# Attention with sinks and a feed-forward layer on one core: key tiles with embedded sinks, one matmul shape, a written weave

## The chip, the cores and the metric

The kernel runs on one core of a Trainium2 chip. The metric is the device time of one execution in microseconds; lower is better. TensorE multiplies matrices into PSUM (eight banks), ScalarE applies functions, VectorE does elementwise work, Pool (GpSimd) does elementwise work on SBUF alone, and SyncE (SP) issues transfers.

## The reference

There are 4 batches of 8 heads with 768 positions and 64 dimensions. Heads 0, 2 and 6 (retrieval) attend to all earlier positions; the other five (streaming) attend to the first 4 positions (the sink) and to the last 64. The attention output, 3072 tokens by 512, goes through a feed-forward layer with a PReLU of one slope per hidden feature:

```
scores = q @ k.T / 8                       # masked: causal, or causal and (sink or window)
a = exp(scores - max) / sum                # per row
x = (a @ v), heads side by side            # 3072 x 512
h = x @ w_in                               # 3072 x 2048
g = max(h, 0) + alpha * min(h, 0)
out = g @ w_out                            # 3072 x 512
```

## The kernel before

The work goes by batch and, in a batch, by four pairs of heads (0,1), (2,3), (4,5), (6,7). `att_load` brings q, k and v of the next pair (SP queue), casts q on ScalarE, k and v on VectorE. `att_pair` transposes q and k (`do_transpose`, L103), so that the two heads of a pair lie on partitions 0 to 63 and 64 to 127. `att_scores` makes transposed scores for each tile of 128 keys: TensorE multiplies 64 partitions of keys by 64 of queries (L118, L138), ScalarE takes the exponential (L120, L140), and a triangular or window mask is multiplied in, on Pool for retrieval heads (L122), on VectorE for streaming heads (L142). A streaming head has its four sink keys apart: two matmuls with 4 key columns (L128) and an exponential of 4 partitions (L130).

`att_av` multiplies by v, which carries a column of ones, into 65 columns for each query tile: full 128-key tiles (L155, L163), for streaming heads also the sink with 4 partitions (L158) and the previous key tile with 64 query columns (L161). VectorE takes the reciprocal of the sum (L166), and ScalarE or VectorE scales (L168, L171). `bridge_gen` transposes the attention output of a batch into `xT` (L211).

The feed-forward layer goes by six chunks of 512 tokens (`moe_chunk_gen`): 16 steps of four matmuls of 512 columns (L234), a scaled copy on ScalarE (L238) and a maximum on VectorE (L239); then four steps of 16 matmuls (L244), a copy (L247) and a store. It has two PSUM banks. The order is partly written and partly found: after each step of attention one step of the feed-forward queue is added, chunk 0 during batch 1, chunks 1 and 2 during batch 2, chunk 3 during batch 3, chunks 4 and 5 at the end; the framework then schedules what is ready, by priority. The weights come first, as fp32 through one staging tile, and VectorE casts them.

Of the kernel before, what the change touches and what calls it, by code (L numbers as in the profile page):

```python
# [9 lines left out]
ALU = mybir.AluOpType  # L10
# [4 lines left out]
def kernel(  # L15
# [18 lines left out]
    NB = S // 128  # L34
# [24 lines left out]
    mwin = const.tile([128, 192], bf16)
    nc.vector.memset(mwin, 1.0)  # L60
    nc.gpsimd.affine_select(mwin, mwin, pattern=[[1, 192]], base=0,
                            channel_multiplier=-1, compare_op=ALU.is_ge, fill=0.0)
    nc.gpsimd.affine_select(mwin, mwin, pattern=[[-1, 192]], base=(WIN - 1),
                            channel_multiplier=1, compare_op=ALU.is_ge, fill=0.0)
    mwin0 = const.tile([128, 192], bf16)
    nc.vector.tensor_copy(mwin0, mwin)
    nc.vector.memset(mwin0[0:NSINK, :], 0.0)

    w_in_b = wpool.tile([128, 4, d_ff], bf16)
    w_out_b = wpool.tile([128, 16, d_model], bf16)  # L70
    alpha_sb = wpool.tile([128, 16], fp32)
    tmpf = wpool.tile([128, 4096], fp32, tag="tmpf")
    for hh in range(2):
        nc.sync.dma_start(tmpf.rearrange("p (a f) -> p a f", a=4),
                          moe_w_in[:, hh * 1024:(hh + 1) * 1024].rearrange("(a p) f -> p a f", p=128))
        nc.vector.tensor_copy(
            w_in_b[:, :, hh * 1024:(hh + 1) * 1024],
            tmpf.rearrange("p (a f) -> p a f", a=4))
# [9 lines left out]
    xT = xpool.tile([128, 4, n_tok], bf16)

    def load_nat(src, key, cvt_eng):  # L90
        nat = qk.tile([128, NB, 2, 64], fp32, tag=f"nat_in_{key}")
        natb = qk.tile([128, NB, 128], bf16, tag=f"nat_b_{key}")
        for hh in range(2):
            nc.sync.dma_start(nat[:, :, hh, :], src[hh].rearrange("(i p) d -> p i d", p=128))
        cvt_eng(natb.rearrange("p i (h d) -> p i h d", h=2), nat)  # L95
        return natb

    def do_transpose(natb, dstT, psum_cvt, bank):
        for half in range(2):
            pt = ps.tile([128, 384], bf16, tag=f"b{bank + half}")  # L100
            for j in range(3):
                i = half * 3 + j
                nc.tensor.transpose(pt[:, j * 128:(j + 1) * 128], natb[:, i, :], ident)  # L103
            psum_cvt(dstT[:, half * 384:(half + 1) * 384], pt)

    def att_scores(hh, h, qT, kT, eT, eTsink):
        retr = RETR[h]
        qTh = qT[hh * 64:(hh + 1) * 64, :]
        kTh = kT[hh * 64:(hh + 1) * 64, :]
        if retr:  # L110
            for j in range(NB):
                W = S - 128 * j
                nh = (W + 383) // 384
                for g in range(nh):
                    w0 = 128 * j + g * 384
                    ww = min(384, S - w0)
# [189 lines left out]
```

## Time and profile before

| what | value |
|---|---|
| median of 3 runs | 422.54 us (420.62 to 426.4) |
| profiled execution, first to last instruction (span) | 420.2 us |
| TensorE busy | 354.1 us (84%) |
| ScalarE busy | 229.3 us (55%) |
| VectorE busy | 193.4 us (46%) |
| Pool busy | 37.4 us (9%) |

The span is the profiled execution's own time; the profile gives no other time for that execution. Busy time of an engine is the union of its instructions. Matmuls are pipelined, so the time from one start to the next is shorter than the length of a matmul, and a TensorE that is always busy need not be at its peak.

### The profile page before, as it was taken

Reading aid. Unit: us, or ns where it says so; the run is one execution under the profiler, and the core shown is the slowest. Engines: PE = TensorE matmul, PEld = TensorE weight load, DVE = VectorE, ACT = ScalarE, POOL = GpSimd, SP = SyncE. Lnnn points to the kernel's source line nnn. Section 1 sums busy time; section 2 is a strip of 40 time slices with the busy share of each in tenths; the row PEclk is TensorE's granted clock in tenths of the full one; section 3 lists DMA queues with packets and bytes.
Section 4 is the critical chain, followed back from the end, with each engine's and each line's share of the span. In section 5 each row is a group of like instructions: output and inputs, shape, how many; then the busy total and the mean of one; then the engine's idle time right before and its main releaser. Section 6 shows DMA issues by size and latency. Waiting matters only on the chain.

```text
span 420.2 us, 5539 instructions
## 1 busy us (share of the span) xinstructions
PE 354.1 (84%) x1890; PEld 156.7 (37%) x1916; DVE 193.4 (46%) x640; ACT 229.3 (55%) x581; POOL 37.4 (9%) x101
## 2 busy tenths in 40 slices
PE   0086788889899788998999999799998998798786
PEld 0033334443335344442343433434344443343332
DVE  3246555546732555665227731567614445512520
ACT  0254566658753565787438753578725565513521
POOL 1020101002010020022000020010300010000000
PEclk9999999999999555898999999799998558999999
DMA  8997975452411551124016051200011000011001
GB/s 230 284 267 220 227 136 114 112 128 62 96 44 75 112 107 30 41 52 114 25 75 114 5 135 50 64 0 2 0 53 50 0 2 0 0 51 50 1 27 75
DMA packets 83692, 33.92 MB, mean 81 GB/s; under 512 B 77520, under 2 KB 77520, under 8 KB 83664
## 3 DMA queue, kind: packets, MB, share of 16 engines
q1 hardware_dynamic: 83664, 33.57, 31.8%
q8 instruction: 15, 0.25, 0.2%
q14 instruction: 13, 0.11, 0.1%
HBM read 27.27 MB, written 6.29 MB: 80 GB/s over the span
## 4 chain that ended last, share of the span: by engine, by line
PE 73%; DVE 10%; ACT 9%; DMA 4%; issue 3%; POOL 1%; ACTq 0%; DVEq 0%
PE po L244 20%; PE psg L234 17%; PE psc L118 6%; PE psc L138 6%; PE pav L155 4%; PE pav L163 4%; PE pav L161 4%; DMA tmpf<-in_moe_w_in_dram 4%; PE pav L158 4%; DVE g L239 4%; ACT hal L238 4%; PE pt L211 3%; PE psc L128 3%; PE pt L103 2%; ACT eTr L120 1%
## 5 line engine op out<-in xcount | busy, mean ns | idle before, releaser
L234 PE MATMUL psg<-xT,w_in_b 128*128 128x512 bf16 x364 | 106.8, 397 | 11.5 <-DVE g L239 10.4
L244 PE MATMUL po<-w_out_b,g 128*128 128x512 bf16 x378 | 89.4, 380 | 1.3 <-DVE g L239 1.0
L239 DVE TENSOR_TENSOR g<-psg,hal 128x512 bf16<-128x512 f32 x96 | 65.7, 686 | 43.9 <-ACT hal L238 43.2
L238 ACT ACTIVATE hal<-psg,alpha_sb 128x512 f32<-128x512 f32 x96 | 66.0, 688 | 32.5 <-PE psg L234 27.8
L166 DVE RECIPROCAL rcp<-pav 128x1 f32<-128x1 f32 x192 | 31.0, 166 | 90.9 <-PE pav L163 51.8
L120 ACT ACTIVATE eTr<-psc 128x384 bf16<-128x384 f32 (+2 forms) x108 | 42.8, 419 | 23.8 <-PE psc L118 22.8
L234 PEld LDWEIGHTS <-w_in_b 128*128 128x128 bf16 x384 | 34.4, 101 | 46.7 <-issue 23.9
L244 PEld LDWEIGHTS <-g 128*128 128x128 bf16 x384 | 34.9, 98 | 41.5 <-issue 3.4
L122 POOL TENSOR_TENSOR eTr<-eTr,mcaus 128x128 bf16<-128x128 bf16 x72 | 32.1, 446 | 201.8 <-ACT eTr L120 201.8
L247 ACT COPY ot<-po 128x512 f32<-128x512 f32 x24 | 14.0, 585 | 62.2 <-PE po L244 53.4
L103 PE MATMUL pt<-ident,natb 128*128 128x128 bf16 x192 | 24.5, 257 | 26.2 <-ACT natb L95 14.1
L142 DVE TENSOR_TENSOR eTs<-eTs,mwin 128x192 bf16<-128x192 bf16 (+1 forms) x120 | 28.6, 249 | 38.6 <-ACT eTs L140 36.2
L140 ACT ACTIVATE eTs<-psc 128x192 bf16<-128x192 f32 (+1 forms) x120 | 36.8, 320 | 15.3 <-PE psc L138 13.1
L118 PE MATMUL psc<-qT,kT 64*128 64x384 bf16 (+2 forms) x108 | 35.5, 349 | 5.1 <-ACT eTr L120 3.8
L138 PE MATMUL psc<-qT,kT 64*128 64x192 bf16 (+1 forms) x120 | 32.2, 289 | 3.3 <-ACT eTsink L130 1.3
L168 ACT ACTIVATE xnat<-pav,rcp 128x64 bf16<-128x64 f32 x96 | 29.8, 314 | 8.0 <-DVE rcp L166 7.0
L155 PE MATMUL pav<-vb,eTr 128*128 128x65 bf16 x252 | 26.2, 215 | 2.0 <-POOL eTr L122 0.8
L211 PE MATMUL pt<-ident,xnat 128*128 128x128 bf16 x96 | 22.0, 273 | 6.6 <-ACT xT L215 4.7
L103 PEld LDWEIGHTS <-natb 128*128 128x128 bf16 x192 | 15.6, 114 | 31.0 <-ACT natb L95 14.3
L158 PE MATMUL pav<-vb,eTsink 4*128 4x65 bf16 x120 | 23.3, 216 | 4.1 <-DVE xnat L171 3.5
L163 PE MATMUL pav<-vb,eTs 128*128 128x65 bf16 x120 | 26.4, 221 | 0.0
L171 DVE TENSOR_SCALAR xnat<-pav,rcp 128x64 bf16<-128x64 f32 x96 | 25.3, 269 | 1.6
(36 smaller groups left out, 247.5 us busy)
## 6 DMA issues: line engine op xcount, KB each, us to landing
nat<-in_q_dram SPq DMA_DIRECT2D x32, 192.0 KB, 3.2
nat<-in_k_dram SPq DMA_DIRECT2D x32, 192.0 KB, 3.6
vnat<-in_v_dram SPq DMA_DIRECT2D x16, 384.0 KB, 3.7
out_dram<-ot SPq DMA_DIRECT2D x24, 256.0 KB, 2.0
tmpf<-in_moe_w_in_dram SPq DMA_DIRECT2D x2, 2048.0 KB, 8.1
tmpf<-in_moe_w_out_dram SPq DMA_DIRECT2D x2, 2048.0 KB, 9.3
alpha_sb<-in_moe_alpha_dram SPq DMA_DIRECT2D x1, 8.0 KB, 8.4
```

What stands on the lines that cost most here:

```text
L103: nc.tensor.transpose(pt[:, j * 128:(j + 1) * 128], natb[:, i, :], ident)
L118: nc.tensor.matmul(psc[:, 0:ww], kTh[:, 128 * j:128 * (j + 1)], qTh[:, w0:w0 + ww], start=True, stop=True)
L120: nc.scalar.activation(eT[j][:, g * 384:g * 384 + ww], psc[:, 0:ww], AF.Exp, scale=scale)
L138: nc.tensor.matmul(psc[:, 0:W], kTh[:, 128 * j:128 * (j + 1)], qTh[:, 128 * j:128 * j + W], start=True, stop=True)
L140: nc.scalar.activation(eT[j][:, 0:W], psc[:, 0:W], AF.Exp, scale=scale)
L155: nc.tensor.matmul(pav, eT[j][:, 128 * (i - j):128 * (i - j) + 128], vbh[:, j, :], start=(j == 0), stop=(j == i))
L158: nc.tensor.matmul(pav, eTsink[:, 128 * i:128 * (i + 1)], vbh[0:NSINK, 0, :], start=True, stop=False)
L163: nc.tensor.matmul(pav, eT[i][:, 0:128], vbh[:, i, :], start=False, stop=True)
L234: nc.tensor.matmul(psg, w_in_b[:, ci, 128 * fj:128 * (fj + 1)], xT[:, ci, t * 512:(t + 1) * 512], start=(ci == 0), stop=(ci == 3))
L238: nc.scalar.activation(hal, psg, AF.Copy, scale=alpha_sb[:, fj:fj + 1])
L239: nc.vector.tensor_tensor(g[:, fj, :], psg, hal, op=ALU.max)
L244: nc.tensor.matmul(po, g[:, fj, 128 * s4:128 * (s4 + 1)], w_out_b[:, fj, :], start=(fj == 0), stop=(fj == 15))
```

## The change

The kernel's body is rewritten. What it computes stays the same.

- All matmuls use the full array. Each of a pair's two heads has its own key tile `kT` with zeros on the other head's 64 partitions, and both use the same `qT`.
- Query tiles start at 0, 128, 252, ... (124 apart, seven of them). Key tiles of a streaming head start 124 apart, and their first four rows are overwritten with the four sink keys (and values), so that sink and window are one matmul; the mask says what counts. A streaming head has 7 score matmuls and 13 value matmuls, a retrieval head 11 and 27.
- Scores of a retrieval head are packed into six pieces of 456 columns, one exponential each; those of a streaming head into three pieces of 384. VectorE multiplies by all masks.
- All seven query tiles of a head are normalised by one reciprocal and one multiplication on VectorE. q, k and the output are evacuated from one transposition bank by VectorE alone.
- q, k and v are cast on Pool, two pairs ahead, and loaded three pairs ahead. The weights are loaded and cast by eight transfers issued from Pool, after the casts of the first two pairs.
- The PReLU is ScalarE's Relu of the negative, then one VectorE instruction (neg times 1 minus alpha, plus h). It has three PSUM banks.
- The order is written out and kept (`manual_schedule`): pieces of attention, and behind them, in equal shares, units of feed-forward: four first-layer matmuls with their two passes, or a quarter of a second-layer sum. Batch 1 gets chunk 0, batch 2 chunk 1 and the first layer of chunk 2, batch 3 the rest of chunks 2 and 3; then chunk 4's first layer, chunk 5's first layer in turn with chunk 4's second, and chunk 5's second.

The added code, cut to its core (what it replaces stands above; setting up masks and buffers is left out):

```diff
+    QS = [0] + [124 * i + 4 for i in range(1, NT)]
+    RW = [S - QS[j] for j in range(6)]
+    RB = [0, 456, 912, 1368, 1824, 2280, RTOT]
+    SLOT = 256
...
+    def load(p):
+        b, c = divmod(p, 4)
+        s = p % NF
+        ha, hb = PAIRS[c]
+        base = (b * H + ha) * S * D
+        nc.sync.dma_start(
+            qf[s].rearrange("p h i d -> p (h i) d"),
+            ap2(q, base, [[D, 128], [128 * D, 12], [1, D]]))
+        for src, dst in ((k, kf[s]), (v, vf[s])):
+            for hh, h in enumerate((ha, hb)):
+                o = (b * H + h) * S * D
+                step = 128 if RETR[h] else 124
+                nc.sync.dma_start(dst[:, 0:6, hh, :], ap2(src, o, [[D, 128], [step * D, 6], [1, D]]))
+                if not RETR[h]:
+                    nc.sync.dma_start(dst[0:24, 6, hh, :], ap2(src, o + 744 * D, [[D, 24], [1, D]]))
...
+        natq[p] = work.tile([128, 6, 128], bf16, tag="qb", name="qb")
+        natk[p] = work.tile([128, 7, 128], bf16, tag="kb", name="kb")
+        nc.gpsimd.tensor_copy(natq[p].rearrange("p i (h d) -> p h i d", h=2), qf[s])
+        nc.gpsimd.tensor_copy(natk[p], kf[s].rearrange("p i h d -> p i (h d)"))
+        nc.gpsimd.tensor_copy(vb[r][:, :, :, 0:D], vf[s])
+        for hh, h in enumerate(PAIRS[c]):
+            if not RETR[h]:
+                kh = natk[p][0:NSINK, :, 64 * hh:64 * hh + 64]
+                nc.gpsimd.tensor_copy(kh[:, 1:7, :], kh[:, 0:1, :].to_broadcast([NSINK, 6, 64]))
+                vh = vb[r][0:NSINK, :, hh, 0:D]
+                nc.gpsimd.tensor_copy(vh[:, 1:7, :], vh[:, 0:1, :].to_broadcast([NSINK, 6, 64]))
...
+    load(0)
+    load(1)
+    load(2)
...
+        nc.vector.memset(kTs[i][0][64:128, :], 0.0)
+        nc.vector.memset(kTs[i][1][0:64, :], 0.0)
...
+    cast(0)
+    cast(1)
+    for n in range(4):
+        nc.gpsimd.dma_start(w_in_b[:, :, 512 * n:512 * (n + 1)],
+                            moe_w_in[:, 512 * n:512 * (n + 1)].rearrange("(a p) f -> p a f", p=128))
+    for n in range(4):
+        nc.gpsimd.dma_start(w_out_b[:, 4 * n:4 * n + 4, :],
+                            moe_w_out[512 * n:512 * (n + 1), :].rearrange("(a p) f -> p a f", p=128))
+    def transposed(nat, n, evac):
+        tr = ps.tile([128, 1024], bf16, tag="tr", name="tr")
+        for i in range(n):
+            nc.tensor.transpose(tr[:, 128 * i:128 * (i + 1)], nat[:, i, :], ident)
+        evac(tr)
+    def Tq(p):
+        transposed(natq[p], 6, lambda tr: nc.vector.tensor_copy(qT[p % NK][:, 0:S], tr[:, 0:S]))
+    def Tk(p):
+        def evac(tr):
+            for hh in range(2):
+                rows = slice(64 * hh, 64 * hh + 64)
+                nc.vector.tensor_copy(kTs[p % NK][hh][rows, :], tr[rows, 0:896])
+        transposed(natk[p], 7, evac)
...
+        lo, hi = RB[n], RB[n + 1]
+        sc = ps.tile([128, 512], fp32, tag=f"sc{n % 2}", name="sc")
+        done = []
+        for j in range(6):
+            a, z = max(lo, RO[j]), min(hi, RO[j] + RW[j])
+            if a < z:
+                c = QS[j] + a - RO[j]
+                nc.tensor.matmul(sc[:, a - lo:z - lo], kt[:, 128 * j:128 * (j + 1)],
+                                 qt[:, c:c + z - a], start=True, stop=True)
+            if lo < RO[j] + RM[j] <= hi:
+                done.append(j)
+        nc.scalar.activation(e[:, lo:hi], sc[:, 0:hi - lo], AF.Exp, scale=scale)
+        for j in done:
+            ej = e[:, RO[j]:RO[j] + RM[j]]
+            nc.vector.tensor_tensor(ej, ej, mr[:, j, 0:RM[j]], op=ALU.mult)
...
+        parts = [(2 * n, 0, 192), (2 * n + 1, 192, 192)] if n < 2 else \
+            [(4, 0, 192), (5, 192, 148), (6, 340, 44)]
+        for j, o, w in parts:
+            nc.tensor.matmul(sc[:, o:o + w], kt[:, 128 * j:128 * (j + 1)],
+                             qt[:, 124 * j:124 * j + w], start=True, stop=True)
+        ev = e[:, 0:6 * SLOT].rearrange("p (s c) -> p s c", c=SLOT)
+        nc.scalar.activation(ev[:, 2 * n:2 * n + 2, 0:192],
+                             sc[:, 0:384].rearrange("p (s c) -> p s c", c=192), AF.Exp, scale=scale)
+        nc.vector.tensor_tensor(ev[:, 2 * n:2 * n + 2, 0:192], ev[:, 2 * n:2 * n + 2, 0:192],
+                                ms[:, 2 * n:2 * n + 2, :], op=ALU.mult)
+    def AV(p, hh):
+        h = PAIRS[p % 4][hh]
+        e, vv = ebuf.pop((p, hh)), vb[p % NV]
+        pav = ps.tile([128, NT, D + 1], fp32, tag=f"pav{hh}", name="pav")
+        for i in range(NT):
+            if RETR[h]:
+                terms = [(RO[j] + QS[i] - QS[j], j) for j in range(min(i, 5) + 1)]
+            elif i == 0:
+                terms = [(0, 0)]
+            else:
+                own = SLOT * i + 4 if i < 6 else 5 * SLOT + 152
+                terms = [(SLOT * (i - 1) + 128, i - 1), (own, i)]
+            for n, (o, j) in enumerate(terms):
+                nc.tensor.matmul(pav[:, i, :], e[:, o:o + 128], vv[:, j, hh, :],
+                                 start=(n == 0), stop=(n == len(terms) - 1))
+        if hh == 0:
+            xn[p] = work.tile([128, NT, 128], bf16, tag="xn", name="xn")
+        rcp = work.tile([128, NT, 1], fp32, tag=f"rcp{hh}", name="rcp")
+        nc.vector.reciprocal(rcp, pav[:, :, D:D + 1])
+        nc.vector.tensor_tensor(xn[p][:, :, 64 * hh:64 * hh + 64], pav[:, :, 0:D],
+                                rcp.to_broadcast([128, NT, D]), op=ALU.mult)
+    def X(p):
+        b, c = divmod(p, 4)
+        nat = xn.pop(p)
+        tr = ps.tile([128, 1024], bf16, tag="tr", name="tr")
+        for i in range(NT):
+            nc.tensor.transpose(tr[:, QS[i]:QS[i] + 128], nat[:, i, :], ident)
+        nc.vector.tensor_copy(xT[:, c, b * S:(b + 1) * S], tr[:, 0:S])
+    n_mm = [0]
+    def mm_bank():
+        n_mm[0] += 1
+        return ps.tile([128, 512], fp32, tag=f"mm{n_mm[0] % 3}", name="mm")
+    def P1(t, f):
+        psg = mm_bank()
+        for c in range(4):
+            nc.tensor.matmul(psg, w_in_b[:, c, 128 * f:128 * (f + 1)], xT[:, c, 512 * t:512 * (t + 1)],
+                             start=(c == 0), stop=(c == 3))
+        neg = work.tile([128, 512], fp32, tag="neg", name="neg", bufs=3)
+        nc.scalar.activation(neg, psg, AF.Relu, scale=-1.0)
+        nc.vector.scalar_tensor_tensor(g_buf[t % 2][:, f, :], neg, oma[:, f:f + 1], psg,
+                                       op0=ALU.mult, op1=ALU.add)
+    po = {}
+    def P2(t, s, quarter):
+        if quarter == 0:
+            po[t] = mm_bank() if t < 4 else ps.tile([128, 512], fp32, tag=f"sc{s % 2}", name="po")
+        for f in range(4 * quarter, 4 * quarter + 4):
+            nc.tensor.matmul(po[t], g_buf[t % 2][:, f, 128 * s:128 * (s + 1)], w_out_b[:, f, :],
+                             start=(f == 0), stop=(f == 15))
+        if quarter == 3:
+            ot = work.tile([128, 512], fp32, tag="ot", name="ot", bufs=3)
+            nc.scalar.copy(ot, po.pop(t))
+            nc.sync.dma_start(out[t * 512 + s * 128:t * 512 + (s + 1) * 128, :], ot)
...
+        seq = [sa[0]] + prev + sa[1:3] + tail + sa[3:5] + nxt[:1] + sa[5:] + nxt[1:] + [sb[0]]
+        seq += [lambda: AV(p, 0)] + sb[1:]
+        return seq
...
+    plan = {1: p1_units(0) + p2_units(0), 2: p1_units(1) + p2_units(1) + p1_units(2),
+            3: p2_units(2) + p1_units(3) + p2_units(3)}
+        pieces = []
+        for p in range(4 * b, 4 * b + 4):
+            pre = [lambda p=p: (load(p + 3) if p + 3 < NP else None)]
+            pre += [lambda p=p: (cast(p + 2) if p + 2 < NP else None)]
+            first = True
+            for piece in pair_pieces(p):
+                pieces.append((pre if first else [], piece))
+                first = False
+        units = plan.get(b, [])
+        lead = 5 if b else 0
+        n = len(pieces) - lead
+        given = 0
+        for i, (pre, piece) in enumerate(pieces):
+            for f in pre:
+                f()
+            piece()
+            due = len(units) * max(0, i + 1 - lead) // n
+            while given < due:
+                units[given]()
+                given += 1
+    AV(NP - 1, 1)
+    X(NP - 1)
+    for u in p1_units(4):
+        u()
+    for u, w in zip(p1_units(5), p2_units(4)):
+        u()
+        w()
+    for u in p2_units(5):
+        u()
```

## Rows read from the trace of the kernel before

**Rows 1.** Busy time and instructions by stretch, granted clock, DMA share, GB/s.

```profile
0.00:23.10 23.10, 1.64 (x12) 1.11 (x12) 7.38 (x11) 2.98 (x4) 1.59 (x9) 1.00 0.90 243
23.10:86.70 63.60, 51.78 (x271) 23.48 (x273) 35.16 (x133) 38.72 (x113) 8.80 (x23) 1.00 0.75 180
86.70:133.60 46.90, 43.90 (x235) 18.41 (x238) 21.55 (x65) 28.44 (x69) 5.46 (x14) 1.00 0.31 78
133.60:167.10 33.50, 28.07 (x173) 14.04 (x171) 18.19 (x82) 20.93 (x63) 3.65 (x9) 0.56 0.38 79
167.10:263.80 96.70, 92.61 (x496) 39.16 (x503) 46.01 (x147) 59.08 (x145) 8.82 (x23) 0.96 0.29 69
263.80:271.00 7.20, 4.79 (x43) 3.04 (x44) 4.15 (x22) 3.69 (x14) 0.00 (x0) 0.75 0.26 75
271.00:317.40 46.40, 44.24 (x243) 18.59 (x246) 22.66 (x69) 28.66 (x70) 5.97 (x14) 0.97 0.06 21
317.40:349.80 32.40, 29.39 (x174) 14.24 (x175) 15.34 (x75) 20.07 (x62) 3.08 (x9) 0.58 0.02 9
349.80:420.20 70.40, 57.66 (x254) 24.66 (x257) 23.00 (x38) 26.73 (x44) 0.00 (x0) 1.00 0.08 30
sum 420.20, PE 354.08 PEld 156.72 DVE 193.44 ACT 229.29 POOL 37.38; mean PE 39.34 PEld 17.41 DVE 21.49 ACT 25.48 POOL 4.15
```

**Rows 2.** Groups of TensorE instructions by shape, 24 to 85 us (batch 0).

```profile
L118 PE MATMUL psc<-qT,kT 64*128 64x384 bf16 x14 | 6.3, 483 | 1.2 <-ACT eTr L120 0.8 <-DVE kT L104 0.2
```

**Rows 3.** The same view, 180 to 260 us (woven).

```profile
L118 PE MATMUL psc<-qT,kT 64*128 64x384 bf16 x11 | 3.6, 343 | 1.3 <-ACT eTr L120 0.8 <-issue 0.5
```

**Rows 4.** TensorE's timeline at five places: start, length, instruction.

```profile
23.14 0.50 PE L118 MATMUL psc<-qT,kT 64*128 64x384 bf16 x1
...
28.57 0.60 PE L155 MATMUL pav<-vb,eTr 128*128 128x65 bf16 x6
...
181.09 0.35 PE L155 MATMUL pav<-vb,eTr 128*128 128x65 bf16 x6
...
188.57 0.45 PE L103 MATMUL pt<-ident,natb 128*128 128x128 bf16 x5
...
236.25 0.20 PE L158 MATMUL pav<-vb,eTsink 4*128 4x65 bf16 x1
236.38 0.22 PE L161 MATMUL pav<-vb,eTs 128*64 128x65 bf16 x1
236.53 0.20 PE L163 MATMUL pav<-vb,eTs 128*128 128x65 bf16 x1
```

**Rows 5.** By stretch: chunk 5's first layer, then its second layer, in the tail.

```profile
382.50:402.50 20.00, 14.79 (x63) 6.07 (x63) 10.37 (x15) 11.43 (x17) 0.00 (x0) 1.00 0.04 14
...
402.50:416.30 13.80, 13.70 (x63) 6.17 (x63) 0.69 (x1) 1.90 (x4) 0.00 (x0) 1.00 0.15 58
```

**Rows 6.** Groups by shape, whole span: busy us, mean ns, idle time before.

```profile
L238 ACT ACTIVATE hal<-psg,alpha_sb 128x512 f32<-128x512 f32 x96 | 66.0, 688 | 32.5 <-PE psg L234 27.8 <-DVE g L239 3.7
L239 DVE TENSOR_TENSOR g<-psg,hal 128x512 bf16<-128x512 f32 x96 | 65.7, 686 | 43.9 <-ACT hal L238 43.2
...
L122 POOL TENSOR_TENSOR eTr<-eTr,mcaus 128x128 bf16<-128x128 bf16 x72 | 32.1, 446 | 201.8 <-ACT eTr L120 201.8
...
L120 ACT ACTIVATE eTr<-psc 128x384 bf16<-128x384 f32 x60 | 28.1, 490 | 19.4 <-PE psc L118 18.9
...
L142 DVE TENSOR_TENSOR eTs<-eTs,mwin 128x192 bf16<-128x192 bf16 x100 | 24.8, 254 | 35.1 <-ACT eTs L140 32.9
...
L104 DVE COPY kT<-pt 128x384 bf16<-128x384 bf16 x32 | 10.7, 351 | 2.1 <-PE pt L103 1.8
...
L95 ACT ACT_TABLE_LOAD x1 | 1.3, 1283 | 11.9 <-DMA nat<-in_q_dram 11.9
L61 POOL TENSOR_SCALAR_AFFINE_SELECT mwin<-mwin 128x192 bf16<-128x192 bf16 x1 | 0.3, 345 | 0.0
```

**Rows 7.** Transfers by line: count, KB each, median us from issue to landing.

```profile
nat<-in_q_dram SPq DMA_DIRECT2D x32, 192.0 KB, 3.2
```

More of the change, by code (lines that the diff above doesn't have):

```diff
@@ L33 @@
     n_tok = B * S
-    NB = S // 128
     scale = 1.0 / (D ** 0.5)
@@ L59 @@
[L59 to L78, printed above, removed]
@@ L88 @@
[L88 to L104, printed above, removed]
@@ L207, in bridge_gen @@
-    def bridge_gen(b):
-        for i in range(NB):
-            for ci in range(4):
-                pt = ps.tile([128, 128], bf16, tag=f"b{ci % 2}")
-                nc.tensor.transpose(pt, x_nat[b][:, i, 128 * ci:128 * (ci + 1)], ident)
-                if ci % 2 == 0:
-                    nc.vector.tensor_copy(xT[:, ci, (b * NB + i) * 128:(b * NB + i + 1) * 128], pt)
-                else:
-                    nc.scalar.copy(xT[:, ci, (b * NB + i) * 128:(b * NB + i + 1) * 128], pt)
-            yield
@@ L251 @@
[L251 to L269 removed]
+    stat = ctx.enter_context(tc.tile_pool(name="stat", bufs=1))
@@ new lines @@
+    work = ctx.enter_context(tc.tile_pool(name="work", bufs=2))
+    ps = ctx.enter_context(tc.tile_pool(name="ps", bufs=1, space=bass.MemoryType.PSUM))
+    ctx.enter_context(tc.manual_schedule())
+    NF, NK, NV, NR, NS = 3, 2, 4, 2, 3
+    qf = [stat.tile([128, 2, 6, 64], fp32, name=f"qf{i}") for i in range(NF)]
+    kf = [stat.tile([128, 7, 2, 64], fp32, name=f"kf{i}") for i in range(NF)]
+    vf = [stat.tile([128, 7, 2, 64], fp32, name=f"vf{i}") for i in range(NF)]
+    vb = [stat.tile([128, 7, 2, 65], bf16, name=f"vb{i}") for i in range(NV)]
@@ new lines, with ap2 @@
+    qT = [stat.tile([128, S + 32], bf16, name=f"qT{i}") for i in range(NK)]
+    kTs = [[stat.tile([128, 7 * 128], bf16, name=f"kT{h}{i}") for h in range(2)] for i in range(NK)]
+    eR = [stat.tile([128, RTOT + 128], bf16, name=f"eR{i}") for i in range(NR)]
+    eS = [stat.tile([128, 6 * SLOT + 64], bf16, name=f"eS{i}") for i in range(NS)]
+    xT = stat.tile([128, 4, n_tok], bf16, name="xT")
+    g_buf = [stat.tile([128, 16, 512], bf16, name=f"g{i}") for i in range(2)]
+    def ap2(t, offset, dims):
+        return bass.AP(t.tensor, t.offset + offset, dims)
@@ new lines @@
+    nc.vector.memset(ms, 1.0)
+    for a, n in ((0, 192), (1, 44)):
+        part = ms[:, 0, :] if a == 0 else ms[:, 5, 148:192]
+        nc.gpsimd.affine_select(part, part, pattern=[[-1, n]], base=63,
+                                channel_multiplier=1, compare_op=ALU.is_ge, fill=0.0)
+        nc.vector.memset(part[0:NSINK, 0:128 if a == 0 else n], 1.0)
+        nc.gpsimd.affine_select(part, part, pattern=[[1, n]], base=0,
+                                channel_multiplier=-1, compare_op=ALU.is_ge, fill=0.0)
```

235 lines of the change are left out of this document (74 added, 161 removed).

## The prediction

> **What bounds the kernel now.** I read the page's busy shares first, then busy time by stretch, then single instructions. The nine stretches of [rows 1] are cut at the first and last feed-forward matmuls of each chunk. TensorE is busy 354.1 of 420.2 us, far more than any other engine, so the first thing to see is what that busy time consists of. Batch 0's attention has 63.6 us to itself, attention of batches 1 and 3 has 33.5 and 32.4 us to itself after its feed-forward chunk ran out, and a tail of 70.4 us has no attention.
>
> Two things in busy TensorE are not arithmetic. The first is the clock. A 64x384 score matmul takes 483 ns in batch 0 [rows 2] and 343 ns in the woven stretch [rows 3]. The granted clock reads 1.00 in batch 0, yet 483 is what the alone stretches with granted 0.56 show too; I take batch 0 to run at the lower level (1.2 GHz) and the 1.00 to be the reading ahead of the first change. The second is the change of array shape. Six matmuls of one shape, 128x65, take 0.35 us together, and one alone 0.20, so one follows another after 0.030 us; a sink, a 64-column and a full-array matmul in turn start 0.13 and 0.15 us apart [rows 4]. Every streaming head goes through these three shapes.
>
> In the tail, 16 first-layer units (four 512-column matmuls each) take 20.0 us, 1.25 each, while 63 second-layer matmuls take 13.70 us, 0.2175 each, so four are 0.87 [rows 5]. The difference is the loop matmul, ScalarE 0.69, VectorE 0.69 [rows 6] over two PSUM banks.
>
> **The change, part by part.** The sum is made against the span of 420.2; the median of the runs, 422.54, is 2.3 above, which I add at the end. A change of about 2% is what measurement can tell from none.
>
> *TensorE work of attention.* Per batch the new kernel has 80 transposes, 68 score matmuls with 13,944 columns (three full heads of 2728, five streaming heads of 1152) and 146 value matmuls of 65 columns. At 2.4 GHz: transposes at 0.06 (five in 0.45, of which the last trails by about 0.2 [rows 4]) give 4.8; the score columns 5.8, with 10 ns a matmul 6.5; the value matmuls at 0.032 give 4.7. That is 16 us a batch, and 32 at 1.2 GHz (value matmuls then 0.07: six in 0.60, less 0.23 [rows 4]). The mask of a retrieval head moves from Pool to VectorE; sinks no longer have matmuls or exponentials of their own.
>
> *Prologue.* Now the first score starts at 23.14 [rows 4], behind a weight transfer and its cast on VectorE. In the new order q, k and v of the first pair (1.18 MB) come first: at the 243 GB/s of the first stretch 4.9 us, with 3.2 us from issue to landing [rows 7] about 8. Then casts on Pool. A Pool instruction with one input took 345 ns for 192 columns, one with two inputs 446 for 128 [rows 6]; the 2560 columns of a pair's casts lie between 4.6 (at 1.8 ns) and 8.9 us (at 3.5), and I take the lower end, the row with one input, much of it fixed cost. The keys are ready some 2 us after landing, transposes and evacuation take 2.5. First score at 12.5 (11 to 18).
>
> *Batch 0.* No feed-forward covers it, as now. A pair with one retrieval head, at 1.2 GHz: nine score pieces 3.75, 20 transposes 2.5, 40 value matmuls 2.9, so about 9 us of matmul. TensorE now goes in a written order, so chains show where too little lies between: last scores, exponential (0.49 for 384 columns), mask (0.25 to 0.5), then the value matmuls of the previous head, about 1 us not covered; normalisation to transposes 0.3; evacuation of queries (0.7 by twice the 351 ns row [rows 6]) to transposes of keys 0.5; mask to the second value matmuls 0.5. That is 11.4; the pair with two streaming heads about 9. Batch 0: 43 us. At the upper clock the pairs fall to about 9, giving 34; that is the lower end. Pool (5 to 9 us a pair) stays below a pair's time.
>
> *Batches 1 to 3.* The 32, 48 and 48 units handed out cost 27.8, 41.8 and 41.8 at 0.87. With attention: 43.8, 57.8, 57.8, together 159. Do the others fit under that? VectorE in batch 2, at most: masks 18 x 0.25 + 15 x 0.51 = 12.1; evacuations (351 ns per 384 columns) 8 x 0.70 + 8 x 0.82 = 12.2; normalisation 8 x 0.77 = 6.2; second pass of the PReLU 32 x 0.69 = 22: 52.5 of 57.8. ScalarE: exponentials 17.8, first pass 22, copies 2.8: 43. So TensorE stays the bound, with VectorE close. Each piece of attention is followed by about one unit, so a chain of exponential and mask has a unit of 0.87 beside it. I add 3 us at each of three starts, where five pieces run uncovered, and 5% (8 us) for waits behind VectorE's queue: 176 (165 to 200) against 263 now (46.9+33.5+96.7+7.2+46.4+32.4).
>
> *Tail.* The last scores, mask, value matmuls, normalisation, transposes and copy leave TensorE about 3.5 us without cover. Then 64 units: with three banks a first-layer unit has 3 x 0.87 = 2.6 us for its loop of 0.87 + 0.2 + 0.69 + 0.69 = 2.45, so it runs at TensorE's rate, and chunk 5 has chunk 4's second layer beside it: 55.7. From the last matmul to the end 3.9 (416.3 to 420.2). Together 63 (61 to 70) against 70.4.
>
> Sum: 12.5 + 43 + 176 + 63 = 294.5, and with the 2.3 **297**.
>
> *Two unpriced things.* The weights come by eight transfers issued and converted by Pool, which no row shows. Beside pair 0 and 1 they cost nothing if Pool is free by about 27 us, when the third pair's casts are due; the upper bound is a rival below, and a gain below nothing is excluded, as nothing reads the weights before batch 1 (about 55 us). The second pass (scalar, tensor, PSUM) is priced like the 686 ns row of the same operands; with a per-partition pointer it may be 0.05 dearer, 1.6 us of VectorE in batch 2, under cover.
>
> **A rule weighed.** All casts go to Pool while VectorE multiplies by masks, both operands in SBUF. In the rows Pool's multiplications (446 ns) and VectorE's masks (254) ran in one kernel and the masks show no long waits on the mean [rows 6]; but Pool was busy only 37 of 420 us [rows 1]. The Trainium skill (SBUF — State Buffer, Who interferes with whom) says that a VectorE instruction with two SBUF inputs contends with a GpSimd instruction that reads SBUF, one blocking the other for its whole length; by it the sum would be some 308, by the rows 297. This is the third rival.
>
> **The rivals.**
> 1. *Upper clock in batch 0 and no loss in the weave*: minus 9 and minus 8, **280**. For it: one array shape, denser matmuls. Against: the alone stretches fell to 0.56 and 0.58 with TensorE 84 to 91% busy [rows 1]. 0.12.
> 2. *Pool is late.* The eight weight transfers stand ahead of the third pair's casts in Pool's order. If Pool is held until their 8.4 MB have moved (243 GB/s: 34 us from about 17), those casts start at 51 instead of 27: **321**. For it: Pool's order. Against: this is the far end of a cost that no row bounds from nearer. 0.13.
> 3. *Pool's reads hold up the masks.* Pool works at least 4.6 us of a pair; if half of a pair's eight masks wait half of a 1 us cast, VectorE gains 2 us a pair: 8 in batch 0, on the path, and in batch 2 60 against 57.8 of TensorE: **308**. 0.08.
> 4. *The written order waits.* The queue of before took what was ready; if the new weave gets no further than the woven stretches of before (46.9 + 96.7 + 46.4 = 190 us for 128 units, 1.48 each), batches 1 to 3 take 199: **320**. For it: VectorE 90% loaded in batch 2. Against: three banks and a unit between pieces. 0.10.
> 5. *Shape was not the price.* If streaming matmuls still start 0.14 apart, 65 x 0.11 and 35 x 0.1 us come back in each of four batches: **339**. Against it the runs of one shape in [rows 4]. 0.03.
> 6. *ScalarE reloads its table between Exp and Relu.* One load took 1283 ns [rows 6]; two for each of 64 woven first-layer units make ScalarE the bound, 73, 125 and 73 us: **408**. Before, Exp and Copy shared one load. 0.02. The Trainium skill (ScalarE: Activation LUTs, Table sets: the hidden batching unit) counts relu among the functions that stand in every set, which speaks against it; no run so far shows Relu.
> 7. *Slower: the lower clock in the woven stretches and the tail.* It falls where small matmuls prevail [rows 1]; if it stayed there from batch 1 on, 159 + 56 us would double: above **500**; it decides from 120 us of cost, a little over half of that time. Against: 1.00, 0.96 and 0.97 in the woven stretches now, where small matmuls had a larger share. 0.03.
>
> **How the numbers follow.** The forecast has 0.47, with 285 to 310 of its own; 0.02 is left for a result near the old time. From 276 to 338 hold the forecast, rivals 2 to 4 and most of rival 1: more than eight in ten, and the bounds of prologue, batch 0 and weave. Faster by over 2%: all but rival 7 and the remainder, 0.95; within 2%: 0.02; slower: 0.03.
>
> **What would show it.** Right: first score near 12.5; value matmuls of streaming heads 0.03 apart (0.07 in batch 0); nine tenths or more busy from some 55 us to the end; in the tail 64 units in 56 us, with TensorE waiting for the second pass almost never. Wrong: waits of query transposes for Pool's casts near 30 us (2), masks far above their length or VectorE busiest in batch 2 (3, 4), table loads beyond the first (6), granted clock near 0.5 after batch 0 (7). The prediction would fail most from VectorE, which has 5 us to spare in batch 2, and from Pool.

## The result and the profile after

The changed kernel takes 293.27 us (median of four, 291.89 to 294.52) against 421.58 before: a ratio of 0.693, 95% interval 0.688 to 0.699. It is 128 us faster; the forecast was 297, range 276 to 338. The profiled execution spans 290.2 us.

Busy time by stretch, kernel after; the stretches are cut at the first score, at the end of VectorE's wait for alpha, where batch 1's first scores start, at two places inside batches 1 to 3, at the last scores' value matmuls, and at the tail's first and last matmul. Columns as in [rows 1]: start and end, length, busy time (and instructions) of TensorE, of its weight loads, of VectorE, ScalarE and Pool, then the granted clock as a share of full speed, the busy share of the transfer engines, and GB/s.

```profile
0.00:12.50 12.50, 1.73 (x13) 1.30 (x13) 7.54 (x32) 1.28 (x1) 8.64 (x29) 1.00 1.11 190
12.50:30.80 18.30, 3.47 (x17) 1.83 (x18) 0.62 (x1) 3.08 (x6) 12.93 (x19) 1.00 1.34 196
30.80:60.40 29.60, 18.81 (x258) 15.33 (x257) 22.60 (x59) 12.97 (x27) 10.42 (x15) 0.88 1.13 206
60.40:110.00 49.60, 44.15 (x407) 26.66 (x414) 37.79 (x82) 25.75 (x51) 19.97 (x30) 0.97 0.62 125
110.00:170.00 60.00, 58.41 (x489) 33.32 (x495) 46.43 (x100) 37.02 (x72) 16.34 (x23) 1.00 0.61 123
170.00:228.30 58.30, 55.75 (x465) 31.74 (x472) 34.77 (x81) 29.96 (x57) 3.67 (x5) 1.00 0.09 33
228.30:230.20 1.90, 0.94 (x21) 0.80 (x20) 0.83 (x2) 0.59 (x1) 0.00 (x0) 1.00 0.10 40
230.20:286.00 55.80, 55.35 (x255) 24.98 (x257) 24.46 (x33) 23.32 (x40) 0.00 (x0) 1.00 0.10 37
286.00:290.20 4.20, 0.00 (x0) 0.00 (x0) 0.00 (x0) 0.48 (x1) 0.00 (x0) 0.83 0.17 62
```

Two things are to be seen against [rows 1]. There is no long stretch with attention alone behind batch 0 any more: from 60.4 to 286.0 TensorE is busy 214.6 of 225.6 us (the five rows from 60.4 on added up), and at full clock almost throughout. And there is a hole: from 12.5 to 30.8 it works 3.5 of 18.3 us, while the transfer engines are busy throughout (a share of 1.34; the times of packets are added up, so it can pass 1).

| stretch | before | forecast | after |
|---|---|---|---|
| to the first score | 23.1 | 12.5 | 12.5 |
| batch 0 | 63.6 | 43 | 47.9 (60.4 - 12.5) |
| batches 1 to 3 | 263.1 | 176 | 167.9 (228.3 - 60.4) |
| tail and end | 70.4 | 63 | 61.9 (290.2 - 228.3) |
| span | 420.2 | 294.5 | 290.2 |

TensorE's timeline, kernel after, at six places (start, length, instruction; in brackets the idle time ahead and what ended it). It answers to [rows 4].

```profile
32.21 0.90 PE L170 MATMUL tr<-ident,kb 128*128 128x128 bf16 x7 [15.77 <-DVE qT L174]
...
33.23 1.69 PE L245 MATMUL pav<-vb,eR 128*128 128x65 bf16 x27
...
41.35 0.98 PE L245 MATMUL pav<-vb,eR 128*128 128x65 bf16 x27
...
109.29 0.33 PE L222 MATMUL sc<-qT,kT 128*128 128x192 bf16 x2
109.45 1.03 PE L286 MATMUL mm<-w_out_b,g 128*128 128x512 bf16 x4
110.31 0.33 PE L222 MATMUL sc<-qT,kT 128*128 128x192 bf16 x3
...
111.54 0.56 PE L245 MATMUL pav<-vb,eS 128*128 128x65 bf16 x13
...
230.24 15.00 PE L272 MATMUL mm<-xT,w_in_b 128*128 128x512 bf16 x66
```

The 13 value matmuls of a streaming head take 0.56 us, 0.03 from one start to the next ((0.56 - 0.2)/12), where sink, previous tile and own tile were 0.13 to 0.15 apart. Two score matmuls of 192 columns take 0.16 before a second-layer unit starts, and that unit 0.86. In the tail, 66 first-layer matmuls run in one piece at 0.227 each.

Groups of instructions by shape, kernel after, answering to [rows 6]:

```profile
L276 DVE SCALAR_TENSOR_TENSOR g<-neg,oma,mm 128x512 bf16<-128x512 f32 x96 | 71.5, 745 | 24.8 <-ACT neg L275 22.4
L275 ACT ACTIVATE neg<-mm 128x512 f32<-128x512 f32 x96 | 57.4, 598 | 44.3 <-PE mm L272 42.9 <-DVE eS L227 0.3
...
L225 ACT ACTIVATE eS<-sc 128x384 bf16<-128x384 f32 x60 | 28.7, 489 | 45.2 <-PE sc L222 45.2
L227 DVE TENSOR_TENSOR eS<-eS,ms 128x384 bf16<-128x384 bf16 x60 | 22.5, 386 | 10.1 <-ACT eS L225 9.9
...
L180 DVE COPY kT<-tr 64x896 bf16<-64x896 bf16 x32 | 19.8, 620 | 6.1 <-PE tr L170 5.6
...
L100 POOL CAST qb<-qf 128x768 bf16<-128x768 f32 x16 | 13.2, 828 | 81.7 <-PE tr L170 73.9 <-DMA out_dram<-ot 7.8
...
L160 POOL DMA_DIRECT2D w_in_b<-in_moe_w_in_dram x4 | 3.1, 796 | 0.0
...
L209 ACT ACT_TABLE_LOAD x1 | 1.3, 1283 | 0.8 <-PEq L369 0.8
```

The second pass of the PReLU takes 745 ns (priced at 690, at most 740), the first 598. Pool casts at 828 ns for 768 columns, 1.08 ns a column, not 1.8. There is still one table load, so Relu and Exp share it.

What held VectorE (waits by releaser: total, times, longest us), kernel after:

```profile
DVE g L276 <- ACT neg L275: 22.4, 33, 1.1
DVE oma L317 <- DMA alpha_sb<-in_moe_alpha_dram: 17.7, 1, 17.7
```

The second line is the hole. VectorE takes its instructions in the order written; `oma` (1 minus alpha) stands behind the first pair's evacuations and ahead of the masks, and alpha's transfer behind the loads of three pairs in SP's queue. No step of the prediction has it.

### The profile page after: what moved, and what is told of

Its sections match the earlier page's. It is cut to its first block, busy times and chain, and to the rows that moved or that the text cites. A ratio compares the mean times of both kernels' runs of the same rounds, so it can differ in the third digit from the quotient of the medians.

```text
span 290.2 us, 5073 instructions
## 1 busy us (share of the span) xinstructions
PE 238.6 (82%) x1916; PEld 136.0 (47%) x1944; DVE 175.0 (60%) x386; ACT 134.4 (46%) x253; POOL 72.0 (25%) x118
## 3 DMA queue, kind: packets, MB, share of 16 engines
q0 software_dynamic: 4224, 4.19, 8.7%
## 4 chain that ended last, share of the span: by engine, by line
PE 64%; DVE 14%; SPq 6%; DMA 5%; POOL 5%; ACT 2%; issue 2%; POOLq 0%; ACTq 0%
PE mm L272 22%; PE mm L286 19%; PE po L286 9%; DVE g L276 6%; DMA vf<-in_v_dram 5%; SPq L85 4%; PE sc L205 4%; PE pav L245 4%; PE tr L170 3%; DVE xn L251 2%; PE tr L259 2%; PE sc L222 2%; DVE kT L180 2%; DVE eS L227 2%; DVE eR L212 2%
## 5 line engine op out<-in xcount | busy, mean ns | idle before, releaser
L272 PE MATMUL mm<-xT,w_in_b 128*128 128x512 bf16 x371 | 95.2, 381 | 1.0 <-issue 0.2
L276 DVE SCALAR_TENSOR_TENSOR g<-neg,oma,mm 128x512 bf16<-128x512 f32 x96 | 71.5, 745 | 24.8 <-ACT neg L275 22.4
L275 ACT ACTIVATE neg<-mm 128x512 f32<-128x512 f32 x96 | 57.4, 598 | 44.3 <-PE mm L272 42.9
L286 PE MATMUL mm<-w_out_b,g 128*128 128x512 bf16 x244 | 63.6, 379 | 0.6
L209 ACT ACTIVATE eR<-sc 128x456 bf16<-128x456 f32 x72 | 38.1, 547 | 32.8 <-PE sc L205 32.7
L225 ACT ACTIVATE eS<-sc 128x384 bf16<-128x384 f32 x60 | 28.7, 489 | 45.2 <-PE sc L222 45.2
L212 DVE TENSOR_TENSOR eR<-eR,mr 128x128 bf16<-128x128 bf16 (+2 forms) x72 | 19.9, 295 | 17.8 <-ACT eR L209 17.6
L286 PE MATMUL po<-w_out_b,g 128*128 128x512 bf16 x125 | 29.9, 379 | 0.1
L205 PE MATMUL sc<-qT,kT 128*128 128x456 bf16 (+8 forms) x132 | 26.0, 284 | 4.4 <-ACT eS L225 2.0
L227 DVE TENSOR_TENSOR eS<-eS,ms 128x384 bf16<-128x384 bf16 x60 | 22.5, 386 | 10.1 <-ACT eS L225 9.9
L180 DVE COPY kT<-tr 64x896 bf16<-64x896 bf16 x32 | 19.8, 620 | 6.1 <-PE tr L170 5.6
L222 PEld LDWEIGHTS <-kT 128*128 128x128 bf16 x140 | 13.1, 102 | 10.8 <-issue 1.4
L205 PEld LDWEIGHTS <-kT 128*128 128x128 bf16 x132 | 11.5, 102 | 11.4 <-issue 1.8
```

The source lines that it names most:

```text
L205: nc.tensor.matmul(sc[:, a - lo:z - lo], kt[:, 128 * j:128 * (j + 1)], qt[:, c:c + z - a], start=True, stop=True)
L209: nc.scalar.activation(e[:, lo:hi], sc[:, 0:hi - lo], AF.Exp, scale=scale)
L212: nc.vector.tensor_tensor(ej, ej, mr[:, j, 0:RM[j]], op=ALU.mult)
L222: nc.tensor.matmul(sc[:, o:o + w], kt[:, 128 * j:128 * (j + 1)], qt[:, 124 * j:124 * j + w], start=True, stop=True)
L225: nc.scalar.activation(ev[:, 2 * n:2 * n + 2, 0:192], sc[:, 0:384].rearrange("p (s c) -> p s c", c=192), AF.Exp, scale=scale)
L227: nc.vector.tensor_tensor(ev[:, 2 * n:2 * n + 2, 0:192], ev[:, 2 * n:2 * n + 2, 0:192], ms[:, 2 * n:2 * n + 2, :], op=ALU.mult)
```

## The experiments

Times are medians; differences are against the changed kernel run again beside the first three (292.5), or against the kernel before where that is the one edited. The runs were made in four groups, on different chips; the kernel before, run in each, took 421.2 to 421.8 us. In the diffs the first line of each pair is the changed kernel's, or that of the kernel before where the text says so.

### The base again

> The changed kernel once more, on the chip of the next three kernels, as their base: 293, within 1%. Its TensorE stands idle from about 16 to 32 us while VectorE waits 17.7 us for alpha.

292.5 us, ratio to before 0.694 (0.687 to 0.701). Same hole: VectorE waited 17.0 us for alpha.

### One shape of matmul: taken back in the changed kernel, and given to the kernel before

```diff
-nc.tensor.matmul(sc[...], kt[:, ...], qt[:, ...], start=True, stop=True)
+nc.tensor.matmul(sc[...], kt[64 * hh:64 * hh + 64, ...], qt[64 * hh:64 * hh + 64, ...], start=True, stop=True)
```

> The score matmuls of the changed kernel use 64 rows of the array (the half of each key tile that isn't zero) in place of 128; the other matmuls stay. Shape theory: each change between the two shapes costs about 0.1 us as in the kernel before (0.13 to 0.15 between starts where one shape needs 0.03); 132 score pieces with two changes each give 20 to 28 us of TensorE, most of it on the path in batches 1 to 3: 308 to 318. Rival (the rows cost nothing, what was saved is the count and the waits): within 2 us of 293.

313.2 us, ratio 0.740 (0.735 to 0.745): 20.7 more. TensorE's timeline of this kernel:

```profile
161.18 1.03 PE L286 MATMUL mm<-w_out_b,g 128*128 128x512 bf16 x4
162.14 0.34 PE L222 MATMUL sc<-qT,kT 64*128 64x192 bf16 x2
162.41 1.04 PE L286 MATMUL mm<-w_out_b,g 128*128 128x512 bf16 x4
```

From the unit's start to the scores' is 0.96 where it was 0.86 (109.45 to 110.31), from the scores to the next unit 0.27 where it was 0.16 (109.29 to 109.45). Each change of shape costs 0.10 us, and two changes for 132 pieces make 26; 20.7 of it comes to the end. The columns streamed are the same, so the rival falls.

The kernel before, with its value matmuls in one shape:

```diff
-nc.tensor.matmul(pav, eTsink[...], vbh[0:NSINK, 0, :], start=True, stop=False)
+nc.tensor.matmul(pav, eTsink[...], vbh[:, 0, :], start=True, stop=False)       # eTsink: 128 partitions, 124 of them zero
-nc.tensor.matmul(pav[0:64, :], eT[i - 1][:, 128:192], vbh[:, i - 1, :], start=False, stop=False)
+nc.tensor.matmul(pav, eT[i - 1][:, 128:256], vbh[:, i - 1, :], start=False, stop=False)   # eT: 64 more columns, zero
```

> The kernel before with its value matmuls in one shape: sinks multiply 128 partitions (zeros in 124), the previous key tile 128 columns (zeros in 64). As many matmuls as before, score matmuls still on 64 rows. Shape theory: 340 value matmuls start 0.03 to 0.07 after one another where they are together, in place of 0.13 to 0.17; changes to score matmuls and transposes stay: 15 to 30 us less, 392 to 407. Rival (the waits of the weave, not the shape, set the time): within 5 us of 421.6.

394.2 us, ratio 0.934 (0.927 to 0.941): 27 us less than the kernel before, with as many matmuls and more zeros multiplied. The shape of the value matmuls alone is worth, in the old schedule, as much as a fifth of the change's 128 us.

### The third PSUM bank: taken from the changed kernel, and given to the tail of the kernel before

```diff
-return ps.tile([128, 512], fp32, tag=f"mm{n_mm[0] % 3}", name="mm")
+return ps.tile([128, 512], fp32, tag=f"mm{n_mm[0] % 2}", name="mm")
```

> The first layer rotates over two PSUM banks in place of three (a second-layer sum takes its turn in the same rotation). By the loop of bank, ScalarE and VectorE (0.87 + 0.2 + 0.6 + 0.75 = 2.4 us for two units), the 16 units of chunk 4 alone take 1.2 each, 5 us more; the woven stretches have 1.1 us from one unit to the next and lose 0 to 0.3 a unit. 298 to 315. Rival (third bank without worth, weave alone did it): within 2 us of 293.

304.9 us, ratio 0.718 (0.711 to 0.724): 12.4 more. TensorE's timeline in the tail of this kernel:

```profile
238.97 1.89 PE L272 MATMUL mm<-xT,w_in_b 128*128 128x512 bf16 x7 [0.61 <-DVE g L276]
241.46 1.89 PE L272 MATMUL mm<-xT,w_in_b 128*128 128x512 bf16 x8 [0.60 <-DVE g L276]
```

Two units every 2.49 us, 1.25 each, with 0.6 idle for VectorE's second pass: the same loop as in [rows 5], though the passes have changed. TensorE's waits for that pass sum to 7.4 us; the other 5 are not in that line.

```diff
-psg = ps.tile([128, 512], fp32, tag=f"b{6 + fj % 2}")
+psg = ps.tile([128, 512], fp32, tag=f"b{6 + fj % 2}" if t < 4 else f"b{(6, 7, 2)[fj % 3]}")
```

This one edits the kernel before.

> The kernel before with one part of the change: chunks 4 and 5 rotate their first layer over three PSUM banks (one that attention no longer uses). If two banks were what made 1.25 us of a unit there: 0.87 to 0.95 a unit, 32 units, 9 to 12 us off 421.6: 410 to 413. Rival (ScalarE and VectorE, 0.69 each, set the rate): no change beyond 2 us.

409.3 us, ratio 0.969 (0.962 to 0.976): 12 less. The last 40 matmuls of chunk 4's first layer, and 62 of chunk 5's, now run without a gap:

```profile
351.88 9.01 PE L234 MATMUL psg<-xT,w_in_b 128*128 128x512 bf16 x40
374.69 13.99 PE L234 MATMUL psg<-xT,w_in_b 128*128 128x512 bf16 x62
```

62 matmuls in 13.99 are 0.226 each, as in the changed kernel. The passes on ScalarE and VectorE are the old ones, so the change of the PReLU had no part in this.

### The weave taken away

```diff
-due = len(units) * max(0, i + 1 - lead) // n
+due = len(units) if i + 1 == len(pieces) else 0
```

> Each batch's feed-forward units come after all of its attention, not between its pieces. TensorE then has nothing to do in the chains of attention, as in batch 0: attention alone took 29 us of batch 0 once alpha was there (30.9 to 60.4, three and a half pairs), so about 34 a batch, where the woven one pays 16 plus 4 for its start: 14 us for each of three batches, with the lower clock up to 20: 330 to 350. Rival (the weave is worth little, since units run at 0.87 either way and chains are short): below 310.

340.6 us, ratio 0.804 (0.799 to 0.810): 48 more. The page's TensorE row and granted clock in 40 slices of 8.5 us, this kernel:

```profile
PE   0501765765679996768899995869999989999994
...
PEclk9999977589799997776999999565999999999999
```

Behind batch 0 there are three dips, in the attention of batches 1 to 3, to 5 to 8 tenths, with a clock of 5 to 9 tenths beside them. So the weave gives 48 us, the largest single part: it fills the chains of attention, and the clock stays up. How much of the 48 is idle time and how much the clock was not separated.

### The written order given back to the scheduler

```diff
-ctx.enter_context(tc.manual_schedule())
```

> The same program with the order found by the framework's scheduler again, in place of the written order. If the written order was needed for the gain: over 310, with TensorE idle more and feed-forward units in other places. Rival (instructions, shapes, banks and casts made the gain): 285 to 300.

282.8 us, ratio 0.667 (0.662 to 0.672): 10 *less*. The written order is no part of the gain; it costs. TensorE's timeline of this kernel in batch 0:

```profile
27.45 0.33 PE L221 MATMUL sc<-qT,kT 128*128 128x192 bf16 x3
27.64 0.38 PE L271 MATMUL mm<-xT,w_in_b 128*128 128x512 bf16 x1
27.91 0.42 PE L244 MATMUL pav<-vb,eS 128*128 128x65 bf16 x8
28.39 0.38 PE L271 MATMUL mm<-xT,w_in_b 128*128 128x512 bf16 x1
```

A first-layer sum needs four quarters of the features, one from each pair, and the scheduler starts on the first quarter while batch 0 is under way. The last value matmuls start at 220.19 us, against 228.31 in the written order. Of these 8 us, 5 are there when chunk 0's second layer starts (84.8 against 89.7 us); the others come later.

### The hole at the start

Theory A is the wait for alpha, theory B the transfer engines. First alpha alone:

```diff
+alpha_sb = wpool.tile([128, 16], fp32, name="alpha_sb")
+nc.sync.dma_start(alpha_sb, moe_alpha.rearrange("(a p) -> p a", p=128))
 load(0)
...
-nc.sync.dma_start(alpha_sb, moe_alpha.rearrange("(a p) -> p a", p=128))
```

> The alpha transfer goes ahead of all loads in SP's queue; nothing else changes. Theory A (VectorE's wait for alpha sets the length of batch 0): the gap from 16 to 32 us goes and the time falls by 10 to 15, to 278 to 283. Theory B (the loads set it: the values of the fourth pair land at 47.7 us whatever VectorE does, and the first feed-forward matmul follows some 18 us later): at most 3 us, 290 to 293.

293.5 us, ratio 0.697 (0.692 to 0.701): no gain. `oma` now ran at 13.41 and the masks followed, but the hole had moved. Pool's timeline of this kernel, with the idle time ahead of each cast:

```profile
33.30 0.82 POOL L100 CAST qb<-qf 128x768 bf16<-128x768 f32 x1 [5.75 <-DMA qf<-in_q_dram]
43.95 0.93 POOL L101 CAST kb<-kf 128x896 bf16<-128x896 f32 x1 [9.83 <-DMA kf<-in_k_dram]
49.70 0.94 POOL L102 CAST vb<-vf 128x896 bf16<-128x896 f32 x1 [4.82 <-DMA vf<-in_v_dram]
```

The fourth pair's q, k and v are late, and TensorE waited 9.0 and 5.9 us for its keys. Theory A falls as the whole cause: the wait for alpha was real, and something as long stood behind it.

Then the weights alone, and both:

```diff
-# the eight weight transfers, right after cast(1)
+if p == 0:
+    pre += [load_w_in]       # after cast(2)
+if p == 1:
+    pre += [load_w_out]      # after cast(3)
```

> The eight weight transfers of Pool go behind the third pair's casts (first layer) and the fourth pair's casts (second layer); alpha stays where it is. Theory A: alpha still stands behind six and more loads in SP's queue, lands some 8 us earlier at most, time 285 to 290. Theory B: the fourth pair's loads no longer share the transfer engines with 8.4 MB of weights and land some 10 us earlier; 280 to 285, unless the weights are then late for the first units.

290.4 us, ratio 0.689 (0.685 to 0.693): 2 less, not clear of the base, and short of the gain that either theory gave. VectorE still waited 7.4 us for alpha, in place of 17.0: the weights had been a part of that wait, too.

> Both moves together. If each hides the other's gain (A and B both true), this falls by 13 to 18, to 275 to 280, and more than the two alone together. Theory A alone: as alpha first, no more. Theory B alone: as weights later, no more.

286.3 us, ratio 0.679 (0.676 to 0.683): 6 less. Each did hide the other's gain, but 6 is less than half of the 13 to 18 expected. One more step, the weights behind the fourth pair's casts (first layer) and the fifth's (second layer); this diff is against the run just before:

```diff
-if p == 0: pre += [load_w_in]
-if p == 1: pre += [load_w_out]
+if p == 1: pre += [load_w_in]
+if p == 2: pre += [load_w_out]
```

> Alpha first, the first layer's weights behind the fourth pair's casts, the second layer's behind the fifth's. Theory B (the transfer engines set batch 0): the first four loads, 4.7 MB at about 200 GB/s, are in by 27 to 30 us; batch 0 then runs at its own chains, about 9 us a pair; first feed-forward unit near 50 in place of 65; 278 to 281. Rival (the casts on Pool or the chains of batch 0 at the lower clock are as long): no better than alpha first and weights later, 285 to 287.

286.7 us, ratio 0.680 (0.674 to 0.685): nothing more, the time that the rival gave, though not for its reason. TensorE's timeline of this kernel where batch 1 begins:

```profile
52.34 0.81 PE L276 MATMUL mm<-xT,w_in_b 128*128 128x512 bf16 x3
...
61.77 0.82 PE L174 MATMUL tr<-ident,kb 128*128 128x128 bf16 x6 [6.47 <-POOL kb L106]
```

The first unit starts at 52.3 in place of 65.5, as theory B said, but then TensorE stands 6.5 us for the next pair's keys; their last copy on Pool comes behind a cast that had waited 8.7 us for its rows. By stretch, the last columns being granted clock, transfer share and GB/s, first the changed kernel:

```profile
20.00:40.00 20.00, 6.17 (x78) 5.11 (x78) 6.56 (x21) 3.88 (x8) 6.34 (x10) 1.00 1.30 194
40.00:60.00 20.00, 12.61 (x181) 10.22 (x180) 15.64 (x38) 8.77 (x20) 10.02 (x14) 0.83 1.09 210
60.00:80.00 20.00, 15.91 (x138) 9.39 (x140) 16.70 (x35) 10.64 (x21) 8.96 (x14) 0.91 1.15 213
80.00:100.00 20.00, 18.36 (x177) 11.10 (x177) 16.18 (x36) 11.08 (x22) 7.39 (x10) 1.00 0.16 39
```

and the one with transfers by need:

```profile
20.00:40.00 20.00, 12.89 (x138) 10.63 (x138) 16.18 (x32) 6.87 (x16) 16.79 (x24) 0.68 1.12 201
40.00:60.00 20.00, 11.19 (x126) 7.42 (x124) 12.41 (x34) 9.35 (x19) 1.76 (x2) 0.84 1.22 199
60.00:80.00 20.00, 17.67 (x164) 10.74 (x168) 15.59 (x29) 11.11 (x22) 12.87 (x19) 0.88 0.99 199
```

In both the engines move about 200 GB/s at a share of about 1 or more up to some 80 us, whatever the order. Moving one transfer forward moves another back. That fits theory B in a stronger form: not the fourth pair's place in the queue, but the sum of weights and rows wanted by then sets the start. The changed kernel's own rows, the weights' queue and the cast that the fourth pair's values release, bear it out:

```profile
q0 software_dynamic: 4224, 4.19, 8.7%
...
47.82 0.94 POOL L102 CAST vb<-vf 128x896 bf16<-128x896 f32 x1 [0.37 <-DMA vf<-in_v_dram]
```

An estimate: four pairs of 1.18 MB and the weights, which the profile counts with 4.19 MB, are 8.9 MB; at the 194 GB/s of the first 40 us that takes 46 us, and the cast started at 47.82. No run made the bytes fewer or the rows longer, so that the sum of bytes is the cause is argued, not shown.

Last, the same transfers with the scheduler's order:

> The same transfers, and the order found by the framework's scheduler. If its gain of 9.7 us over the written order came from filling the waits for transfers in batch 0 (it started single first-layer matmuls at 27.6 us), little of it is left: 275 to 280. If it came from the starts of batches 1 to 3, where the written order runs five pieces uncovered, it adds up: 268 to 273.

280.3 us, ratio 0.663 (0.656 to 0.669): 6 less than the same transfers in the written order, and the lowest median, though not clear of the free order alone (0.662 to 0.672). It lies just above the first of the two ranges, but that range was for little of the gain being left, and two thirds of it are: 6.4 of 9.7 us. So part of it lies outside the first waits. When chunk 0's second layer starts, 3.7 us are there (80.0 against 83.7); which of the later starts give the rest isn't settled.

## Why the prediction was right, and where only its sum was

**The base: shape, loop and clock as what TensorE's busy time held.** Right. The change of shape was priced at 0.10 to 0.12 us from [rows 4], and both kernels show it, 0.10 a change in the one and 27 us for value matmuls in the other. The loop over two banks was read from [rows 5], and adding the bank alone gave 12 us.

**Prologue 12.5.** Right, with wrong terms: the casts were priced at 1.8 ns a column and took 1.08, while q, k and v took until 8.7 us, and VectorE, which was still clearing buffers, evacuated the queries only at 10.36. That they met at 12.5 is luck in part.

**Batch 0: 43, measured 47.9.** This is the step that failed, and the total hides it. What it left out is the transfer engines: only the first pair's 1.18 MB had a price, the other pairs none, and the weights stood only in rival 2, as something that holds Pool. Behind these transfers alpha came late, and TensorE waited 16 us (32.21). What it had too dear is the attention itself: from 30.8 to 60.4, 29.6 us hold pairs 1 to 3 and the rest of pair 0, some 8.5 us a pair in place of 11.4 and 9, partly because the clock was not at the lower level throughout (27 value matmuls took 1.69 us at 33.23 and 0.98 at 41.35), partly because the scores of pair 0 were done by then. A wait of 16 us left out and attention 11 us too dear met; that the stretch came out 5 us off is luck.

**Batches 1 to 3: 176, measured 167.9.** The TensorE work (159) was right; what I added for waits was too much. Batches 2 and 3 took 58.5 us each where 57.8 is work, so a start and the weave's waits together cost 1 us by the sum, and 1.6 and 2.6 by TensorE's idle time:

```profile
111.30:169.80 58.50, 56.94 (x479) 32.56 (x486) 45.00 (x96) 36.21 (x69) 15.67 (x22) 1.00 0.63 126
169.80:228.30 58.50, 55.93 (x465) 31.83 (x473) 34.97 (x82) 30.13 (x57) 3.67 (x5) 1.00 0.09 33
```

VectorE has 45.0 of batch 2's 58.5, below the 52.5 given as the most, where a key evacuation was taken at 0.82 us and took 0.62 (L180). Batch 1 took 51 (60.4 to 111.3), 7 more than its 43.8 of work: TensorE was idle for 1.9 us up to the first unit (65.48), where the clock was granted 0.81, and for 3.6 us after it. In all 8.5 us came to the 159 of work, where I had added 17.

**Tail: 63, measured 61.9.** The units are right (55.7, measured 55.8) and the end nearly so (3.9 and 4.2); the uncovered end of attention took 1.9 us in place of 3.5.

**The rivals.** Pool late (2): its issue of a weight transfer took 0.80 us, and the third pair's casts stood at 21.96 us, so Pool was not the thing; the transfers themselves were, as far as the runs on the hole show. Table loads (6), shape without a price (5), the lower clock (7), the waits of the weave (4): not seen. Pool's reads and the masks (3) were seen, and small. Masks by line in the kernel after (minimum, median, longest ns), and one of the longest with the cast beside it:

```profile
L212 DVE TENSOR_TENSOR eR<-eR,mr x72: 210/226/990, 30.9 to 222.7; 128x128 bf16<-128x128 bf16 x24, 128x132 bf16<-128x132 bf16 x12, 128x136 bf16<-128x136 bf16 x12, 128x140 bf16<-128x140 bf16 x12
...
L227 DVE TENSOR_TENSOR eS<-eS,ms x60: 346/352/834, 34.5 to 227.3; 128x384 bf16<-128x384 bf16 x60
...
54.94 0.99 DVE L212 TENSOR_TENSOR eR<-eR,mr 128x128 bf16<-128x128 bf16 x1
...
55.03 0.82 POOL L100 CAST qb<-qf 128x768 bf16<-128x768 f32 x1
```

Some masks take up to a cast longer than the median; with means of 295 and 386 ns that is at most 7 us above the medians over all (72 x 0.069 and 60 x 0.034; the wider shapes among the first take a little of it by themselves). The Trainium skill's rule (SBUF — State Buffer, Who interferes with whom), that the two block each other for an instruction's length, agrees with these lengths: all 18 masks that last longer than 232 ns (L212) or 359 ns (L227) overlap a cast or copy on Pool in the trace; the 98 masks that overlap none stay within these lengths, and so do 16 that overlap one.

**What the forecast did not ask.** It took the written order as a cost of waits (rival 4) or of nothing; that a free order of the same program would be 10 us faster was not among the cases.

Of the 128 us, by what one part is worth when it alone is taken back or added: the weave 48, one shape at least 21 (scores) and 27 (values, in the old schedule), the third bank 12, the first score 10.6 earlier (23.1 to 12.5). These overlap, since each was measured with the others as they stood, so they are not terms of one sum. What the embedded sinks, the packed exponentials, the normalisation by heads and the casts on Pool are worth was tried by no run.

## What to carry to other kernels

Price every engine at the start, the transfer engines too: sum the bytes that must be in by each stage, divide by the rate of a row with the same packets, and compare with the stage; two waits of the same length hide one another, so removing one can show nothing (alpha first: 293.5 against 292.5). Count changes of matmul shape (0.10 us each here) and PSUM banks against the loop of a sum (matmuls, both passes): each can be tried alone with a few lines. Interleave dense matmuls with latency-bound work (48 us here), but try the scheduler's own order beside a written one; here it was 10 us faster.

## What the runs showed of the hardware

- A granted clock of 1.00 at the start of a trace can be no reading at all: in the kernel before a 64x384 score matmul took 483 ns there [rows 2], and 493 ns between 135 and 166 us, where the clock was granted 0.5 for the most part; in the kernel after 27 value matmuls took 1.69 us at 33.23, with 1.00 shown up to there, 0.057 from start to start, against 0.03 at 41.35.
- With rows of 256 bytes and the weights beside them, the transfer engines moved 190 to 213 GB/s at a share of 1 or more, up to 80 us. The Trainium skill (DMA: Bandwidth & Descriptors, Specifications) gives 512 bytes as the least transfer for line rate; no run here changed the size of a row.
- An 8 KB transfer of single values held VectorE for 17.7 us. The wait was 7.4 us with the weights' transfers later, and none with alpha first in SP's queue, so it came from what stood ahead of it and from what moved beside it.
